# A chunked delta rule before an FFN: chunks 0 and 1 solved by 16x16 blocks and three accumulating products

## The chip, the cores and the metric

The kernel runs on one core of a Trainium2 chip. Its time is the device time of one execution in microseconds; a single program on one core, so there is no second core to compare. The engines are TensorE (PE; its weight loads are PEld in the profile), VectorE (DVE), ScalarE (ACT), GpSimd (POOL) and SyncE (SP), which here only issues DMAs.

## What is computed

For each of 4 batches and 8 heads, 768 steps with a state of 48x48, then an FFN over the 3072 rows (384 wide, 1536 hidden):

```python
k_n = k / (norm(k, axis=-1) + 1e-06)
for t in range(S):
    y[:, :, t] = q[:, :, t] @ state
    v_old = state.T @ k_n[:, :, t]
    state = state + beta[:, :, t] * outer(k_n[:, :, t], v[:, :, t] - v_old)
...
xn = x / rms(x) * rms_g
out = (silu(xn @ w_gate) * (xn @ w_val)) @ w_out
```

k, q, v, beta and the output are float32 in the kernel; the three weight matrices arrive as float64 and are converted on the chip.

## The kernel before

**Chunks.** The 768 steps are 12 chunks of 64 (C). Inside a chunk the state's corrections solve a unit triangular system of 64x64 for each of the 32 heads: with N the negative, strictly lower part of K K^T scaled by beta, the rows wanted are M r, where M is the inverse times beta and r is v less what the old state gives. `prep` (from L598) makes M, `recur` (from L844) applies it: `mr` (M r, L912), the output y (`pu`, L926), the state (`ku`, L963), the root mean square and the transposed, scaled rows `xf`, the FFN's input.

**prep.** K is scaled by 1/norm (in chunk 0 on VectorE, L646, and before that the raw scores are scaled by it, L624), transposed on TensorE (`turn`, L529) and multiplied by itself (`scores`, L552). The two diagonal 32x32 blocks of each head go through DRAM (`dkk`) into `at_`, one block per partition. VectorE then substitutes: scaling by beta (L671), pairs of rows (L696 to L706), and 15 steps of a product (L718) and a sum (L724) on `acc`. The result goes through DRAM (`dx`) into `mt` (the two diagonal blocks of M) and `x2bd`. For chunks 0 and 1 (`early`) TensorE turns the first block (L776) into `m1bd`; two products (L800, L824) make the block below the diagonal of M. For chunks 2 to 11 `m1bd` is loaded by DMA instead.

**The FFN.** Chunks 0 and 1 are multiplied plainly (`ffn_plain`: up L1101, down L1083), in two halves of the hidden width, so that half the weights suffice at first. From chunk 2 on, weight sums are formed (`factors`, `out_factors`), and the FFN runs with fewer products (L1194, L1251).

**Weights.** 18 loads of 768 KB arrive in three raw buffers in `more`. Each is converted by one ScalarE step (L473) and three VectorE steps (L461 to L469); for the first three (NPE) TensorE adds the two parts by an identity product (L486, L487) and ScalarE copies them out (L491), for the others VectorE adds them (L494).

**What sets the order.** Every operation is first given to a planner (`Plan`) with an engine, a price, a priority and its dependences; the planner writes out one fixed order for each engine. A DMA's `after` is a time in the planner's own clock before which it isn't placed; on the chip the queue takes the DMAs in their written order, each as soon as its semaphores allow. Most DMAs are issued by SP, a few of chunk 0 by ScalarE's queue. Until 70 us of the planner's clock the gaps on TensorE are filled with products of the identity (`filler`, L1354), which compute nothing that is used. TensorE takes its instructions in order, fillers among them.

Of the kernel before, what the change touches and what calls it, by code (L numbers as in the profile page):

```python
# [11 lines left out]
FP32 = mybir.dt.float32  # L12
# [6 lines left out]
C = 64  # L19
W = 32  # L20
DP = 64
# [30 lines left out]
def fillers(a, b):  # L52

    if a == 0.0:
        return [4, 4, 4, 1]
    n, t = [], a
    while t < b - 0.3:
        n.append(4 if b - t > 1.5 else 2 if b - t > 0.9 else 1)
        t += 0.22 * n[-1] + 0.02
    return n  # L60
# [195 lines left out]
def kernel(  # L256
# [42 lines left out]
    bk = sbt("bk", [128, W])  # L299
    mhalf = sbt("mhalf", [128, 2])  # L300
    zero = sbt("zero", [128, 1])
# [8 lines left out]
    NPE, NRAW, NCV = 3, 3, 2  # L310
# [20 lines left out]
    kraw = pt  # L331
    at_ = sbt("at", [128, W, W])
    acc = sbt("acc", [128, 4, W // 2, W])
    xs_ = [acc[:, 1], wflat[:, 2048:2560].rearrange("p (i t) -> p i t", t=W), wflat[:, 2560:3072].rearrange("p (i t) -> p i t", t=W)]
    xt_ = acc[:, 2].rearrange("p i t -> p (i t)").rearrange("p (k i) -> p k i", i=W // 2)
    m1bd = sbt("m1bd", [128, 16, 2, W])
    x2bd = sbt("x2bd", [128, 8, 4, W])
    mt = [sbt("mt", [128, 16, C]), wflat[:, 1024:2048].rearrange("p (x t) -> p x t", t=C)]
# [25 lines left out]
    dx = [dram.tile([2, 2, 16, W, W], FP32, name=f"dx{i}") for i in range(2)]  # L364
    dxt = [dram.tile([W, 2, 16, W], FP32, name=f"dxt{i}") for i in range(2)]
# [14 lines left out]
    def due(c, lead):  # L380

        return (64.0 - min(lead, 64.0)) if c == 0 else (90.0 if c == 1 else 160.0 + PERIOD * (c - 2)) - lead


    def setup():
# [24 lines left out]
        for keys, t in (  # L410
            ([("m1bd", g, bb) for g in range(2) for bb in range(2)], m1bd),
            ([("x2bd", y_) for y_ in range(4)], x2bd),
        ):
            n = 1
            for e in t.shape[1:]:
                n *= e
            P.add("POOL", 0.05 + 0.0009 * n, lambda t=t: nc.gpsimd.memset(t, 0.0), 1, w=keys)
        for i in range(2):
            P.add("POOL", 1.0, lambda t=mt[i]: nc.gpsimd.memset(t, 0.0), 1, w=[("mt", i, h_, bb, g) for h_ in range(3) for bb in range(2) for g in range(2)])

    def load_small():
        for i in range(8):
            src = beta.rearrange("b (y g) (c i t) -> i g (b y) c t", i=2, g=2, t=W)[i // 2 % 2, i % 2]
            dma(beta_b[16 * i : 16 * i + 16], src, 0.5, w=[("beta", i)], work=0.2, after=7.5)
        dma(g_sb, moe_rms_g.rearrange("(t p) -> p t", p=128), 1, w=["g"], after=8.0)
# [6 lines left out]
    def weights():  # L432
# [14 lines left out]
        for n, (dst, src, keys) in enumerate(todo):  # L447
# [4 lines left out]
            dma(rdst, src, (0.1 if n == 0 else 3 + 2 * n), w=[("raw", i)], dur=0.7, work=3.06, after=(7.5, 5.0, 19.2, 27.2, 24.5, 33.3, 47.0)[n] if n < 7 else 48.8)  # L452
# [25 lines left out]
            if n < NPE:  # L478
                for x_ in range(2):
                    ps = Group()  # L480
                    cut = slice(2 * x_, 2 + x_)
                    flat = slice(512 * x_, 512 + 256 * x_)
                    m = 512 - 256 * x_
# [5 lines left out]
                    P.add("PE", 0.0035 * m, s6, pr, r=cvk + cak + ["ident"], w=[("cvp", n, x_)], ps=ps, size=8)  # L489
                    done.append(("cv", n, x_))  # L490
                    P.add("ACT", A(m), lambda dst=dst[:, cut], ps=ps, m=m: nc.scalar.copy(dst, ps.t[:, 0:m].rearrange("p (a n) -> p a n", n=256)), pr, r=[("cvp", n, x_)], w=[done[-1]], last=ps)  # L491
# [9 lines left out]
    def load(c, what):  # L501
        t0 = c * C
        pk, pq, pv = ((-5, 1, 12), (5, 29, 36))[c] if c < 2 else (due(c, 150), due(c, 99), due(c, 70))
        if "q" in what and c > 1:
            for d, eh, g, th in itertools.product(range(2), repeat=4):
# [3 lines left out]
                dma(q2t[r0 : r0 + 32, :, g, th, 0 : e1 - e0], src, pq, w=[q2k[8 * d + 4 * eh + 2 * g + th]], work=0.2, after=53.2)  # L509
# [88 lines left out]


    def prep(c):  # L600
        early = c < 2
        pr = 8.0 if c == 1 else due(c, 110)
        if c == 0:
            pr = 0.0
# [785 lines left out]
```

## Time and profile before

| What | us |
|---|---|
| median of 3 runs | 705.16 (703.76 to 706.37) |
| the profiled execution | 705.78 |
| its span | 704.1 |
| TensorE busy | 687.3 |
| VectorE busy | 556.3 |
| first up-projection of the FFN (first row of L1101) | 73.37 |

In the rows of the profile, a line is: the kernel's line, engine, operation, output <- inputs, shape and count. TensorE's timeline gives the start, the length of a merged piece, and in brackets how long the engine was idle before it and what ended that. A float32 product is two TensorE records, each with a weight load of its own. The weight loads by form give busy us and the mean ns of one. Clock and matmul ends are modelled in the profile, so pitches are read from starts.

### The profile page before, as it was taken

Reading aid. Unit: us, or ns where it says so; the run is one execution under the profiler, and the core shown is the slowest. Engines: PE = TensorE matmul, PEld = TensorE weight load, DVE = VectorE, ACT = ScalarE, POOL = GpSimd, SP = SyncE. Lnnn points to the kernel's source line nnn. Section 1 sums busy time; section 2 is a strip of 40 time slices with the busy share of each in tenths; the row PEclk is TensorE's granted clock in tenths of the full one; section 3 lists DMA queues with packets and bytes.
Section 4 is the critical chain, followed back from the end, with each engine's and each line's share of the span. In section 5 each row is a group of like instructions: output and inputs, shape, how many; then the busy total and the mean of one; then the engine's idle time right before and its main releaser. Section 6 shows DMA issues by size and latency. Waiting matters only on the chain. (4 is left out here: it accounts for less than half of the span.)

```text
span 704.1 us, 23246 instructions
## 1 busy us (share of the span) xinstructions
PE 687.3 (98%) x9956; PEld 623.0 (88%) x9956; DVE 556.3 (79%) x1149; ACT 307.3 (44%) x735; POOL 139.8 (20%) x140
## 2 busy tenths in 40 slices
PE   9998989999999999999999999899999999999997
PEld 6657767777789999999999999899999999999997
DVE  4799979999799869789579669979769779648373
ACT  5434643444335446345445444246445435236241
POOL 4202111104212033213113033303033210000000
PEclk9999999999999999999999999999999999999999
DMA  7967796743612531633611442442541430210000
GB/s 144 239 129 170 154 254 127 165 69 58 111 23 44 93 58 24 104 66 54 105 34 24 81 77 48 80 76 40 83 74 22 74 71 3 45 33 2 23 1 24
DMA packets 232791, 54.67 MB, mean 78 GB/s; under 512 B 221936, under 2 KB 225008, under 8 KB 232688
## 3 DMA queue, kind: packets, MB, share of 16 engines
q1 hardware_dynamic: 227840, 52.27, 39.1%
q10 hardware_dynamic: 4848, 0.92, 0.8%
q8 instruction: 78, 1.28, 0.8%
q14 instruction: 25, 0.20, 0.1%
HBM read 40.83 MB, written 12.32 MB: 75 GB/s over the span
## 5 line engine op out<-in xcount | busy, mean ns | idle before, releaser
L1194 PE MATMUL bank<-xf,w_in 128*128 128x128 f32 x1440 | 180.4, 277 | 2.5 <-ACT tmp L1206 2.5
L1194 PEld LDWEIGHTS bank<-xf,w_in 128*128 128x128 f32 x1440 | 169.8, 192 | 5.3 <-ACT tmp L1206 2.7
L1204 DVE TENSOR_TENSOR tmp<-tmp,bank 128x512 f32<-128x512 f32 x180 | 121.3, 682 | 57.7 <-PE bank L1194 51.8
L1194 PE MATMUL bank<-xf,more 128*128 128x128 f32 x960 | 124.3, 277 | 0.0
L1194 PEld LDWEIGHTS bank<-xf,more 128*128 128x128 f32 x960 | 115.3, 192 | 1.6 <-issue 0.2
L1206 ACT COPY tmp<-bank 128x512 f32<-128x512 f32 x120 | 68.7, 585 | 93.0 <-PE bank L1194 66.0
L1210 ACT ACTIVATE tmp<-tmp 128x256 f32<-128x256 f32 x120 | 49.9, 418 | 94.7 <-DVE tmp L1204 94.4
L724 DVE TENSOR_REDUCE acc<-acc 128x30 f32<-128x90 f32 (+4 forms) x180 | 85.1, 473 | 6.2
L574 POOL TENSOR_TENSOR knrm<-ksum,half 128x16 f32<-128x16 f32 x12 | 35.6, 2968 | 166.7 <-DVE ksum L573 166.7
L718 DVE TENSOR_TENSOR acc<-acc,at 128x60 f32<-128x60 f32 (+4 forms) x180 | 62.4, 346 | 4.6 <-POOL at L701 1.7
L1251 PE MATMUL bank<-wo_sb,hf 128*128 128x192 f32 x360 | 63.9, 327 | 1.2 <-ACT xf L1038 1.0
L1251 PEld LDWEIGHTS bank<-wo_sb,hf 128*128 128x128 f32 x360 | 58.2, 190 | 1.8 <-ACT xf L1038 1.2
L1211 DVE TENSOR_TENSOR hf<-tmp 128x256 f32<-128x256 f32 x120 | 50.4, 435 | 6.5 <-ACT tmp L1210 5.9
L1354 PE MATMUL bank<-ident 128*128 128x128 f32 (+2 forms) x156 | 44.7, 433 | 1.4 <-POOL ident masks.py:199 1.4
L1354 PEld LDWEIGHTS bank<-ident 128*128 128x128 f32 x156 | 26.6, 196 | 18.1 <-issue 15.2
L671 POOL TENSOR_TENSOR at<-at,beta_b 128x1024 f32<-128x1024 f32 x8 | 19.6, 2450 | 105.1 <-DMA at<-dkk 51.8
L1260 DVE TENSOR_TENSOR tmp<-tmp,bank 128x192 f32<-128x192 f32 x30 | 10.5, 350 | 31.9 <-PE bank L1251 30.8
L1083 PE MATMUL bank<-wo_sb,hf 128*128 128x384 f32 x96 | 34.9, 495 | 0.0
L1101 PE MATMUL bank<-xf,w_in 128*128 128x256 f32 x144 | 34.1, 386 | 0.6 <-ACT xf L1038 0.6
L1101 PE MATMUL bank<-xp,w_in 128*128 128x256 f32 x144 | 33.5, 382 | 0.0
L745 POOL COPY acc<-acc 128x128 f32<-128x128 f32 x40 | 21.4, 564 | 60.7 <-DVE acc L724 60.2
L1101 PEld LDWEIGHTS bank<-xf,w_in 128*128 128x128 f32 x144 | 26.5, 190 | 5.4 <-ACT xf L1038 0.9
(167 smaller groups left out, 1018.9 us busy)
## 6 DMA issues: line engine op xcount, KB each, us to landing
at<-dkk SPq DMA_DIRECT2D x23, 256.0 KB, 4.4
more<-in_moe_w_val_dram SPq DMA_DIRECT2D x6, 768.0 KB, 5.8
more<-in_moe_w_gate_dram SPq DMA_DIRECT2D x6, 768.0 KB, 7.3
more<-in_moe_w_out_dram SPq DMA_DIRECT2D x6, 768.0 KB, 8.8
vt<-in_v_dram SPq DMA_DIRECT2D x24, 192.0 KB, 4.4
out_dram<-tmp SPq DMA_DIRECT2D x48, 96.0 KB, 2.2
k<-in_k_dram SPq DMA_DIRECT2D x23, 192.0 KB, 4.0
mt<-dx SPq DMA_DIRECT2D x84, 32.0 KB, 2.1
```

Source lines behind the costliest of these rows:

```text
L574: P.add("POOL", 2.95, lambda: nc.gpsimd.tensor_tensor(out=knrm[i2], in0=ksum[i2], in1=half, op=ALU.pow), pn, r=[("ksum", i2), "half"], w=[ ...
L718: nc.vector.tensor_tensor(out=acc[:, 1:3, 0:n, j + 2 : W].rearrange("p a i t -> p i a t"), in0=acc[:, old, 0:n, j : j + 2, None].to_broadc ...
L724: nc.vector.tensor_reduce(out=acc[:, new, 0:n, j + 2 : W], in_=acc[:, lo : lo + 3, 0:n, j + 2 : W].rearrange("p a i t -> p i t a"), axis=A ...
L1083: nc.tensor.matmul(po[p].t[:, 0:DM], hf[:, spot(f), 128 * p : 128 * p + 128], wo_sb[:, spot(f)], start=(f == f0), stop=(f == f1 - 1), skip ...
L1101: nc.tensor.matmul(ps.t[:, TOK * side : TOK * side + TOK], w_in[:, side, h_, 3 * t + i_, n : n + 128], x_[:, 2 * t : 2 * t + 2].rearrange( ...
L1194: nc.tensor.matmul(g.t[:, 128 * z : 128 * z + 128], fac[:, side, 128 * f : 128 * f + 128], xf[:, xs], start=(begin and z == 0), stop=False ...
L1204: P.add("DVE", V(512), lambda t=t, g=g: nc.vector.tensor_tensor(out=t, in0=t, in1=g.t, op=ALU.add), -1, r=[g], w=[tk], last=g)
L1206: P.add("ACT", A(512), lambda t=t, g=g: nc.scalar.copy(t, g.t), -1, r=[g], w=[tk], last=g)
L1210: P.add("ACT", A(256), lambda t=t: nc.scalar.activation(out=t[:, 0:256], in_=t[:, 0:256], func=ACTF.Silu), -1, w=[tk])
L1211: P.add("DVE", V(256), lambda t=t, f0=f0, p=p: nc.vector.tensor_tensor(out=hf[:, spot(f0) : spot(f0) + 2, 128 * p : 128 * p + 128], in0=t[ ...
L1251: nc.tensor.matmul(g.t[:, 0:192], a_[:, f], b_[:, f], start=(begin and f == 0), stop=(f == 5), skip_group_check=True)
L1354: nc.tensor.matmul(warm[:, 0 : 128 * w_].rearrange("p (w n) -> p w n", n=128), ident, ident[:, None, :].to_broadcast([128, w_, 128]))
```

## The change

Chunks 0 and 1 get a function of their own, `prep16`; `prep` keeps chunks 2 to 11 and loses its `early` branches. The strict part below the 16x16 diagonal blocks is not inverted any more: with D the inverse of the diagonal blocks and E = D N, both of each head's 64x64, u = D r is followed by three rounds of u = D r + E u, each written as a product with the last change that accumulates in the same bank. Two heads share one 128x128 block-diagonal tile (`nbd` for N, `ebd` for E).

```diff
+L = 16
-        return [4, 4, 4, 1]                      # fillers before the first work
+        return [4, 4, 1]
-    NPE, NRAW, NCV = 3, 3, 2
+    NPE, NRAW, NCV = 4, 3, 2
...
-due(c): 160.0 + PERIOD * (c - 2)
+due(c): 162.0 + PERIOD * (c - 2)
...
-        beta after=7.5, g after=8.0
+        beta after=2.0, g after=27, and b16: beta by 16x16 blocks, two ScalarE copies
-        weights after=(7.5, 5.0, 19.2, 27.2, 24.5, 33.3, 47.0)[n] if n < 7 else 48.8
+        weights after=(1.4, 29.5, 35.9, 33.7, 36.0, 38.0, 39.5)[n] if n < 7 else 52.9
-        q, k of chunk 1 and v: after=1.4, 27.2; 8.6; 34.4, 41.2; later q and k 53.2
+        q, k of chunk 1 and v: after=18.2, 45; 5.9; 14.0, 44.7; later q and k 46.5
```

Beside the diff's own lines above, the changed tables are given in one line each. The planner's price of a TensorE conversion also changes. The new function, cut:

```diff
+    def prep16(c):
+        if c == 0:
+            turn(kn, kt[0], ktk, kkeys + kp, pr, True)          # K not scaled by its norm
+            ps = scores(kt[0], kt[0], pr, ktk, ...)
+            kraw = -scores                                      # one VectorE, one ScalarE copy
+            bk = (1/norm by block) * (1/norm by block) * b16[:, 0]
+        else:
+            kd scaled by krec on GpSimd; turn; scores; n0 = -scores (ScalarE)
+        for g in range(2):
+            dma(dk[g].rearrange("x j t -> j x t"), full[64 * g : 64 * g + 64], ...)      # 256 KB each
+            nbd[rows, :, 64 * g : 64 * g + 48] = full[rows, :, 0:48] * below             # GpSimd
+        if c == 0:
+            vt = vt * knrm[0]                                   # VectorE, 128x768
+        for r0, b0, n in place:                                 # four loads of 16x16 blocks
+            dma(a16[c][r0 : r0 + W], dk...[:, b0 : b0 + L, b0 : b0 + L], ...)
+        scale (128x256), share1, share3, share2 (128x128)       # VectorE
+        for j in range(0, L - 2, 2):                            # seven steps
+            n, m = j + 2, L - 2 - j
+            nc.vector.tensor_tensor(out=acc[:, 1:3, 0:n, cols]..., op=ALU.mult)
+            nc.vector.tensor_reduce(out=acc[:, new, 0:n, cols], ..., op=ALU.add)
+        spread: two ScalarE copies into x16[c]
+        for r0, b0, n in place:
+            dma(dm...[:, b0 : b0 + L, b0 : b0 + L], x[r0 : r0 + W], ...)     # dm was zeroed by one 512 KB store
+        for g in range(2):
+            dma(dg[c][64 * g : 64 * g + 64], dm[g].rearrange("x s t -> s x t"), ...)
+        if c:
+            four more loads of dm into mt[1]
+        for h in range(2):
+            for bb in range(2):
+                for y_ in range(4):
+                    nc.tensor.matmul(ps.t[:, n : n + 64], nbd[:, x_], dg[c][:, x_])       # coupling
+            ebd <- ps, on the diagonal; half by VectorE, half by ScalarE (64x512 each)
```

In `recur`, for c < 2 (chunk 0 in two halves h, chunk 1 in one):

```diff
+        def couple(h, t):
+            for p in h:
+                for bb in range(2):
+                    for y_ in range(4):
+                        nc.tensor.matmul(psu[bb, p].t[:, n : n + 48], ebd[:, x_], t[:, x_], start=False, stop=True, ...)
...
         for h in halves:
+            first product: first_rows(h) for c == 0 (dg and v), mr(h) otherwise
+            evacuate(h, c > 1)                                  # u <- bank
+            if c > 1:
+                continue
+            for n in range(3):
+                P.add("PE", 0.7 * len(h), couple(h, zb if n else u_), ...)
+                if n < 2:
+                    change(h)                                   # zb = bank - u, VectorE
+                if n == 0:
+                    evacuate(h, False, ("ACT", "ACT"))
+            evacuate(h, True)
```

Removed for chunks 0 and 1: the 32x32 substitution, `dkk`, `dx`, `x2bd`, `turn_m11` (L776), the two merging products (L800, L824) with their copies, and in chunk 0 the second transposes and scores of the scaled K. GpSimd clears the shared tile `mx` (ebd, and m1bd with x2bd for the later chunks) again after chunk 1.

## Prediction

> **What bounds the kernel now.** I read the page first, then the table of engine time by stage, TensorE's timeline over the first 110 us, VectorE's timeline beside it, and the weight loads by form.
>
> ```profile
> PE 687.3 (98%) x9956; PEld 623.0 (88%) x9956; DVE 556.3 (79%) x1149; ACT 307.3 (44%) x735; POOL 139.8 (20%) x140
> ```
>
> TensorE is busy for 98% of the span, but not with work all the time. Its timeline tells the two apart:
>
> ```profile
> 28.97 9.85 PE L1354 MATMUL bank<-ident 128*128 128x512 f32 x28
> ...
> 46.02 8.13 PE L1354 MATMUL bank<-ident 128*128 128x512 f32 x24
> ...
> 61.11 1.41 PE L912 MATMUL bank<-vt,mt 64*64 64x48 f32 x64
> ...
> 73.37 4.15 PE L1101 MATMUL bank<-xf,w_in 128*128 128x256 f32 x18 [0.64 <-ACT xf L1038]
> ...
> 103.15 0.32 PE L926 MATMUL bank<-u,pt 64*64 64x48 f32 x5 [2.20 <-issue]
> ```
>
> L1354 is filler. Up to the first up-projection at 73.37 TensorE spends 41 us on fillers (177 blocks of 128 columns), 7 us idle and about 25 us on work; in the 630.7 us behind it, it is idle for 11. So the end moves with two things only: when the first up-projection starts, and how much TensorE work lies behind it. The start waits for chunk 0's substitution on VectorE, between these rows (13.3 us; scaling and pairs from 25.39 make it 16.6), and for its stores and loads:
>
> ```profile
> 28.72 0.22 DVE L718 TENSOR_TENSOR acc<-acc,at 128x60 f32<-128x60 f32 x1
> ...
> 41.73 0.28 DVE L724 TENSOR_REDUCE acc<-acc 128x30 f32<-128x90 f32 x1
> ```
>
> **The price that decides.** The rest of the triangle is now three products with ebd (`couple`), each a full 128x128 weight tile with only 48 moving columns, and the tiles come from products with nbd (64 moving columns). Every fp32 product is two records with a weight load each. No row of before has a full tile with so few columns, so I bound it. These are weight loads by form, with the mean in ns last:
>
> ```profile
> L1194 PEld LDWEIGHTS bank<-xf,w_in 128*128 128x128 f32 x1440 | 169.8, 192 | 5.3 <-ACT tmp L1206 2.7 <-issue 1.0 <-ACT tmp L1296 0.2
> L552 PEld LDWEIGHTS bank<-kt 64*64 64x64 f32 x832 | 13.7, 134 | 4.4 <-issue 2.7 <-ACT kt L541 0.7 <-DVE tmp L1204 0.5
> L800 PEld LDWEIGHTS bank<-m1bd,kk 128*32 128x32 f32 x352 | 5.4, 109 | 2.9 <-issue 2.0 <-DMA q<-in_q_dram 0.2
> ```
>
> 192, 134 and 109 ns for 128, 64 and 32 columns: 0.86 ns per column, so 128 columns need some 0.11 us. A matmul that follows other work, its load unhidden, against one in a run (timeline):
>
> ```profile
> 26.28 0.70 PE L486 MATMUL bank<-xf,ident 128*128 128x512 f32 x1
> ```
>
> ```profile
> 16.86 0.59 PE L487 MATMUL bank<-more,ident 128*128 128x512 f32 x1
> ```
>
> Again 0.11 us is what an exposed load adds. And from the chain of waits the pitch in a run:
>
> ```profile
> 493.00 0.87 PE bank L529 x8
> ...
> 664.01 21.44 PE bank L1194 x192
> ...
> 685.45 1.95 PE bank L1251 x12
> ```
>
> 0.109 us for 128 moving columns (L529), 0.1625 for 192 (L1251): 0.00084 per column. Lower end, the load fully hidden: 0.042 for 48 columns, 0.055 for 64. Upper end, each record waits for its load: 0.1117, L1194's pitch (load and stream not overlapped at all is excluded: L1194 would then be near 0.22). There are 96 + 32 new products, half per chunk: 192 + 64 records, 11.5 us by the lower end, 28.6 by the upper. I take the upper: the load's slope and the exposed 0.11 are both of full tiles, and a next load cannot hide behind a 0.04 us stream.
>
> The Trainium skill, "TensorE: Matmul & The Clock Gate", has both rules: section "LDWEIGHTS (loading the stationary operand)" gives columns / 1.2 in ns, 107 for 128 columns, and the table in "Back-to-back issue gap" gives about 60 cycles, 25 ns, for up to 64 moving columns. Estimates from that page: 27.3 us for the new products by the first rule, 6.4 by the second, which would make the whole 708 or 688; the rows above side with the first, against this change.
>
> **Part by part, up to the first up-projection.** TensorE's queue in the changed kernel's instruction order, up to its first w_in product, holds:
> - the start, 1.4, and 9 filler blocks at the first fillers' slow rate (13 took 5.5): 3.8;
> - 104 more filler blocks at 0.217 (45 took 9.7 from 28.97): 22.6;
> - old work by its rows: eight k, q and k1 transposes each 0.87, scores 1.09 + 1.05 + 1.1, norms 0.2, two conversions 5.3 (26.28 to 28.97 is one), first product 1.08, y 1.1, state 0.7, transposes 0.66: 14.9. Chunk 0's second transposes and scores, L776, L800 and L824 are gone;
> - new, chunk 0's half: 14.3.
>
> That is 57.0 without any wait. Now the chain. K goes out unscaled after one 0.69 copy behind the scores (near 10.3) instead of two 0.65 scalings behind the reciprocal (12.25). The two 256 KB stores should land in about 4 (a 192 KB k load: 4.0), by 14.5. The four block loads move 64-byte pieces, 512 each: nearest are dxt (1024 such pieces, 2.7) and the contended block load on ScalarE's queue (6.0).
>
> ```profile
> dxt<-acc SPq DMA_DIRECT2D x20, 64.0 KB, 2.7
> ...
> at<-dkk ACTq DMA_DIRECT2D x1, 256.0 KB, 6.0
> ```
>
> Two of them stand on ScalarE's queue behind w_in copies that wait for the first weight conversion, and v, the zeros and q (1.3 MB) follow on SP, so I take 20 (18 to 22). Substitution: scale and pairs 1.2 (256 elements 0.41, L1109), then seven steps of 28 to 64 outputs at the pitch of L718 with L724 (0.55 at 30, 0.69 at 56): 4.5. Stored out near 26.4, landed 29.6, back as one tile 34 (4.0 again). TensorE's queue reaches the coupling at 33, so this chain and the fillers end nearly together. The three rounds are then TensorE's own: one half's 1.8 us of products covers the other half's change (2 x 0.36 on VectorE) and copies (2 x 0.4 on ScalarE); at the lower price some 0.8 a round would be bare. First y product near 52.6; from there 8.4 by L988, L1013, L1021, L1034 and L1038 (10.7 in before, with a 1.15 stop and fillers). So the first up-projection is at **61**, that is 4 of waits on 57, where before has 5.5.
>
> Covered: VectorE's v scaling (1.1), the b16 copies, GpSimd's nbd products (four of about 1.5, L646) and its memsets end before 17; if a nbd product ended after 33 the coupling would slip by as much. The block zeros after chunk 1 (1.9) are wanted only near 140. Loads released anew: weight 1 now goes out behind the tile load, near 30, and lands at 36 to 41; VectorE wants it near 43; each us later moves the start by one. Weights 2 and 3 go near 33; in VectorE's order chunk 1's substitution (5.8, saving 11 there) stands before their conversions, done by 62 and 64 against a need at 65 and 69.
>
> **Behind it.** 630.7, plus a conversion that was done before (n=2) and one moved from VectorE (n=3), 5.3; q1's transposes and scores, 2.0; chunk 1's new products 14.3, less L776, L800 and L824, 2.2; less 2.0 for the stop at 103.15, which stands behind runs of small records that become fewer (0 at the other end): 648.1. Chunks 2 to 11 keep their instructions. VectorE's net saving, about 17 us (two substitutions from 33.2 to 11.4, 10 of new copies, changes and v scaling against 5 of old ones), is off the path: TensorE covers it.
>
> **Sum:** 61 + 648.1 = 709.1 against a span of 704.1, so 5.0 us longer. The profiled execution took 705.78 in all; the median of the runs is 705.16, so I say 710.2.
>
> **Rivals.**
> - *The load hides* (faster): the streams set the pitch, 0.042 and 0.055. The queue then holds 48.5, waits grow to 5, start 53.5; behind it 639.6. 693.1, or 694.2 as a median. For: rows with smaller tiles pass at 0.017. Against: four of them load side by side, and the 0.11. Between the ends the sum is a line, and it crosses 704.1 where the 256 records average 0.091 us; below that the change wins.
> - *No difference*: the price as forecast, but no waits up to the start (57) and 3.7 less idle behind it: 703.4, 704.5 as a median. For: VectorE has 17 us less to do. Against: 5.5 of waits in before.
> - *The stores and loads come late*: the block loads or the tile at the contended 6.0 to 7.0, the tile back near 39. Start 66, 714.1, 715.2 as a median. For: v, zeros and q in the same queues. Against: no weight load beside the chain.
>
> **Chances:** forecast 0.50, load hides 0.20, no difference 0.17, late 0.13. The forecast alone reaches from 706 to 714, and 0.06 of it lies below 708.7. Half a per cent, 3.5 us, is about what a measurement of this kernel can tell from no change: slower 0.57, same 0.23, faster 0.20. The range runs from 694 to 717, taking in both ends of the price.
>
> **What will show it.** The pitch of the 48-column records: 0.11 or 0.04. The first up-projection at 61. VectorE's first substitution in under 6 us, from about 20. TensorE idle for 9 to 12 behind the start. I am wrong if those records pass below 0.09, or if TensorE idles anew behind the start.

## The result and the profile after

| | before | after |
|---|---|---|
| median of 4 runs each, us | 704.46 (703.03 to 706.37) | 733.46 (731.79 to 736.18) |
| ratio | | 1.0414 (95%: 1.0366 to 1.0461) |
| the profiled execution, its span | 705.78, 704.1 | 736.18, 734.5 |
| first up-projection (first row of L1101, L1282 after) | 73.37 | 84.09 |
| behind it | 630.7 | 650.4 |
| mean granted clock | 0.999 | 0.967 |

Slower by 29 us; 710.2 was forecast. Behind the first up-projection the forecast was 648.1, and it is 650.4. The miss is in the start: 84.09 instead of 61. These are two lines of the page of after, TensorE's busy time and the granted clock in 40 slices of 18 us.

```profile
PE 719.2 (98%) x9858; PEld 658.1 (90%) x9858; DVE 537.6 (73%) x1129; ACT 304.9 (42%) x733; POOL 148.9 (20%) x147
...
PEclk9965899899999999999999999999999999999999
```

The share of busy time is 98% again and tells nothing. The second line does: the clock is at 6 and 5 tenths in the third and fourth slice, where it was full in before. TensorE's timeline of after shows what ran there:

```profile
41.58 5.12 PE L780 MATMUL bank<-mt,wsum 128*128 128x64 f32 x32 [1.78 <-DMA mt<-dm]
46.63 3.65 PE L1056 MATMUL bank<-vt,mt 64*64 64x48 f32 x64
...
50.80 6.90 PE L1067 MATMUL bank<-u,mx 128*128 128x48 f32 x32
...
58.91 6.90 PE L1067 MATMUL bank<-state,mx 128*128 128x48 f32 x32
...
66.16 6.90 PE L1067 MATMUL bank<-state,mx 128*128 128x48 f32 x32
...
84.09 4.15 PE L1282 MATMUL bank<-xf,w_in 128*128 128x256 f32 x18
...
109.09 3.68 PE L780 MATMUL bank<-kk,wsum 128*128 128x64 f32 x32
...
115.14 3.77 PE L1067 MATMUL bank<-u,mx 128*128 128x48 f32 x32
```

L1067 is `couple`, a round of 32 records. For chunk 1 (115.14) it takes 3.77, for chunk 0 6.90, nearly twice as long, with nothing idle inside. The engine time by stage, cut at the edges at which the clock changes, confirms that this is the clock (after the busy times: granted clock, DMA share, GB/s):

```profile
40.30:43.72 3.42, 2.14 (x19) 2.17 (x20) 0.06 (x1) 0.00 (x0) 0.00 (x0) 1.00 1.11 312
43.72:47.13 3.41, 3.41 (x25) 3.29 (x26) 1.01 (x2) 0.58 (x1) 0.28 (x1) 0.50 0.93 263
...
53.96:57.37 3.41, 3.41 (x18) 3.41 (x17) 0.62 (x2) 0.54 (x2) 0.00 (x0) 0.50 0.00 0
...
74.44:77.85 3.41, 3.41 (x51) 1.65 (x53) 0.00 (x0) 0.76 (x2) 0.00 (x0) 0.50 0.88 158
77.85:81.26 3.41, 3.41 (x100) 2.77 (x96) 1.69 (x7) 3.21 (x13) 1.10 (x2) 1.00 0.24 46
```

From 43.72 to 77.85, ten stretches of 3.41 us, the clock is exactly half. (Between the ends of each trace, every piece that the clock stays at one value is a multiple of 3.41 us long, at a phase of its own.) Half clock also comes for one stretch at 16.4, at 118.8 (behind a stretch that a round of chunk 1 filled without a gap) and for two at 142.7. Undisturbed, the weight load is what the forecast said. The loads by form, mean ns last but for the idle times:

```profile
L1375 PEld LDWEIGHTS bank<-xf,w_in 128*128 128x128 f32 x1440 | 170.7, 192 | 3.4 <-DVE tmp L1385 1.0 <-issue 0.6 <-ACT tmp L1387 0.4
...
L1067 PEld LDWEIGHTS bank<-state,mx 128*128 128x128 f32 x64 | 13.9, 333 | 0.0
...
L1067 PEld LDWEIGHTS bank<-r,mx 128*128 128x128 f32 x64 | 7.4, 192 | 0.3
```

192 ns for chunk 1's tiles, as for any full tile; 333 for chunk 0's. The second thing in the start is VectorE's timeline:

```profile
11.80 1.79 DVE L614 TENSOR_SCALAR knrm<-knrm 128x16 f32<-128x16 f32 x1
...
13.80 2.48 DVE L503 SCALAR_TENSOR_TENSOR tmp<-more,tmp 128x768 f32<-128x768 uint32 x1
...
25.75 0.42 DVE L705 TENSOR_TENSOR at<-at,bk 128x256 f32<-128x256 f32 x1 [8.10 <-DMA at<-dfull]
...
31.39 0.27 DVE L748 TENSOR_REDUCE acc<-acc 128x28 f32<-128x84 f32 x1
```

The substitution itself takes 5.9 us (25.75 to 31.66), as forecast, but starts at 25.75 instead of 20, after 8.1 us of waiting for its loads. And two operations in front of it are odd: L614 takes 1.79 for 128x16 elements (0.16 for chunk 1, at 31.58). The DMA view (median us from issue to landing last):

```profile
dfull<-pt SPq DMA_DIRECT2D x1, 256.0 KB, 4.9
...
mt<-dm ACTq DMA_DIRECT2D x1, 256.0 KB, 5.8
at<-dfull SPq DMA_DIRECT2D x6, 32.0 KB, 5.2
dm<-at SPq DMA_DIRECT2D x6, 32.0 KB, 1.9
at<-dfull ACTq DMA_DIRECT2D x2, 32.0 KB, 4.9
```

SP issued its two block loads of chunk 0 at 17.06, ScalarE's queue its two at 20.12, behind the copies of the first conversion (L524), the second of which starts at 20.05.

### The profile page after: what moved, and what is told of

Read it like the earlier page. It is cut to its first block, busy times and chain, and to the rows that moved or that the text cites. A ratio compares the mean times of both kernels' runs of the same rounds, so it can differ in the third digit from the quotient of the medians.

```text
span 734.5 us, 23017 instructions
## 1 busy us (share of the span) xinstructions
PE 719.2 (98%) x9858; PEld 658.1 (90%) x9858; DVE 537.6 (73%) x1129; ACT 304.9 (42%) x733; POOL 148.9 (20%) x147
## 4 chain that ended last, share of the span: by engine, by line
PE 85%; DVE 7%; DMA 4%; SPq 2%; ACT 1%; issue 1%; ACTq 0%; DVEq 0%
PE bank L1375 36%; PE bank L1432 19%; PE bank L1282 6%; PE bank L1067 4%; PE bank L995 3%; PE bank L589 3%; PE bank L1264 2%; SPq L389 2%; PE bank L1077 2%; PE bank L1042 1%; PE bank L566 1%; PE bank L780 1%; DMA more<-in_moe_w_gate_dram 1%; PE bank L520 1%; DVE acc L887 1%; PE bank L1215 1%
## 5 line engine op out<-in xcount | busy, mean ns | idle before, releaser
L1375 PEld LDWEIGHTS bank<-xf,w_in 128*128 128x128 f32 x1440 | 170.7, 192 | 3.4 <-DVE tmp L1385 1.0
L1375 PE MATMUL bank<-xf,more 128*128 128x128 f32 x960 | 125.9, 278 | 0.0
L887 DVE TENSOR_REDUCE acc<-acc 128x30 f32<-128x90 f32 (+4 forms) x150 | 71.0, 473 | 5.2
L881 DVE TENSOR_TENSOR acc<-acc,at 128x60 f32<-128x60 f32 (+4 forms) x150 | 51.0, 340 | 6.6 <-POOL at L864 5.0
L1282 PE MATMUL bank<-xp,w_in 128*128 128x256 f32 x144 | 35.6, 402 | 0.0
L1282 PE MATMUL bank<-xf,w_in 128*128 128x256 f32 x144 | 35.3, 396 | 0.0
L1282 PEld LDWEIGHTS bank<-xp,w_in 128*128 128x128 f32 x144 | 28.6, 202 | 5.5 <-DVE hf L1290 0.3
L1282 PEld LDWEIGHTS bank<-xf,w_in 128*128 128x128 f32 x144 | 28.0, 198 | 5.4 <-issue 0.2
L907 POOL COPY acc<-acc 128x128 f32<-128x128 f32 x40 | 19.6, 521 | 64.5 <-DVE acc L887 64.3
L1538 PE MATMUL bank<-ident 128*128 128x512 f32 (+2 forms) x90 | 30.4, 484 | 1.4 <-POOL ident masks.py:199 1.4
```

Source lines behind the costliest of these rows:

```text
L881: nc.vector.tensor_tensor(out=acc[:, 1:3, 0:n, j + 2 : W].rearrange("p a i t -> p i a t"), in0=acc[:, old, 0:n, j : j + 2, None].to_broadc ...
L887: nc.vector.tensor_reduce(out=acc[:, new, 0:n, j + 2 : W], in_=acc[:, lo : lo + 3, 0:n, j + 2 : W].rearrange("p a i t -> p i t a"), axis=A ...
L1282: nc.tensor.matmul(ps.t[:, TOK * side : TOK * side + TOK], w_in[:, side, h_, 3 * t + i_, n : n + 128], x_[:, 2 * t : 2 * t + 2].rearrange( ...
L1375: nc.tensor.matmul(g.t[:, 128 * z : 128 * z + 128], fac[:, side, 128 * f : 128 * f + 128], xf[:, xs], start=(begin and z == 0), stop=False ...
L1538: nc.tensor.matmul(warm[:, 0 : 128 * w_].rearrange("p (w n) -> p w n", n=128), ident, ident[:, None, :].to_broadcast([128, w_, 128]))
```

## The experiments

**Theories.** *A*: records that are bound by their weight load and stream few columns lower the clock by themselves. *B*: the stops of TensorE ahead of the coupling (1.62 and 1.78 us) lower it, whatever is multiplied. *C*: the clock has no part; the products' price and the late chain are the cause. "Start" is the first up-projection in the profiled execution, "behind" the rest of its span, before on the same chips 704.93 to 706.11. In e2 to e7, e11 and e12 VectorE, ScalarE, GpSimd and SP have the instructions of after in the same order, so that only TensorE's products differ.

| run | median, us | ratio, 95% | start | behind |
|---|---|---|---|---|
| after | 733.46 | 1.037 to 1.046 | 84.09 | 650.4 |
| e4_no_idle | 717.03 | 1.013 to 1.020 | 67.43 | 648.2 |
| e5_wide | 715.91 | 1.012 to 1.021 | 66.01 | 648.3 |
| e11_wide64 | 715.3, 715.7, 731.4, 735.4 (each) | | 66.89 | 647.0 |
| e3_fill_between | 734.97 | 1.038 to 1.047 | 82.73 | 649.8 |
| e6_twice48 | 747.59 | 1.055 to 1.062 | 95.33 | 651.7 |
| e7_twice64 | 729.56 | 1.030 to 1.037 | 77.19 | 650.1 |
| e2_tiles64 | 707.70 | 1.000 to 1.005 | 65.36 | 643.1 |
| e12_nbd_late (the same program as e2) | 706.43 | 1.000 to 1.004 | 63.66 | 643.0 |
| e8_sp_loads | 710.66 | 1.005 to 1.010 | 60.67 | 651.5 |
| e9_npe3 | 706.64 | 0.998 to 1.004 | 62.99 | 642.6 |
| e10_combined | 711.95 | 1.006 to 1.011 | 62.67 | 647.8 |
| e13_nbd_after | 704.97 | 0.996 to 1.000 | 69.58 | 636.7 |
| e14_v_after | 705.75 | 0.997 to 1.002 | 69.68 | 636.0 |
| e15_v_after_npe3 | 709.70 | 1.004 to 1.010 | 70.56 | 635.4 |

### No stop ahead of the coupling

```diff
             def coupling(h=h, ps=ps):
+                if not c and not h:
+                    filler([4, 4, 4])
```

> Three filler blocks (2.6 us) go ahead of chunk 0's coupling, where TensorE stops for 1.8 us. Theory A (the run of few-column products does it): the clock falls all the same, at most one window of 3.4 us later, and the time stays within 731 to 736. Rival B (the stop does it): the clock holds through the coupling and the rounds, 17 us go and about 0.8 comes: 717 to 720.

717.03: B's number. TensorE's timeline of this run:

```profile
41.12 3.68 PE L782 MATMUL bank<-mt,wsum 128*128 128x64 f32 x32
...
47.05 3.67 PE L1069 MATMUL bank<-u,mx 128*128 128x48 f32 x32
...
51.28 3.67 PE L1069 MATMUL bank<-state,mx 128*128 128x48 f32 x32
...
55.08 3.67 PE L1069 MATMUL bank<-state,mx 128*128 128x48 f32 x32
...
67.43 4.15 PE L1284 MATMUL bank<-xf,w_in 128*128 128x256 f32 x18
```

The same products, each round 3.67 instead of 6.90, the start 16.7 us earlier, the rest of the span nearly as it was (648.2 for 650.4). So the clock is worth 16.4 us of the 29 (733.46 less 717.03, the three fillers included), and C falls. A, as I had put it, falls too: the same run of few-column products passed at full clock.

### More columns under the same weight loads

```diff
-    nc.tensor.matmul(ps.t[:, n : n + 64], nbd[:, x_], dg[c][:, x_])
+    nc.tensor.matmul(ps.t[:, n0_ : n0_ + 128], nbd[:, x_], dg[c].rearrange("p x t -> p (x t)")[:, f0 : f0 + 128])
...
-    nc.tensor.matmul(psu[bb, p].t[:, n : n + 48], ebd[:, x_], t[:, x_], ...)
+    nc.tensor.matmul(psu[bb, p].t[:, n : n + 128], ebd[:, x_], t.rearrange("p x e -> p (x e)")[:, f0 : f0 + 128], ...)
```

> Chunk 0's products with ebd and nbd each stream 128 moving columns instead of 48 or 64 (the neighbouring columns too, so the values of chunk 0's rows are not the reference's); the number of records and of weight loads is the same, and each does more. Theory A (the clock is halved because too few columns stream under each weight load): at full clock a record with 128 columns passes in 0.11 to 0.12 us, as one with 48 does, so with more work per record the kernel gets faster: the clock stays above 0.9, a round takes 3.6 to 3.9 instead of 6.9, first up-projection near 67 to 70, 716 to 720 in all. Rival C, or any in which the products' own cost is what lengthens the start: 733 or more, since no record gets cheaper by streaming more. Rival B (the stop ahead of the coupling): half clock at 43.7 still, rounds of 6.9, 733.

715.91, though each product streams twice to nearly three times as much and the stop of 1.74 us ahead of the coupling is still there. The clock stays full, a round takes 3.74. That is A's number, and B falls: the stop alone does not do it either. Engine time in the stretch with the stop, to be set beside 40.30:43.72 of after:

```profile
37.47:40.88 3.41, 2.15 (x19) 2.18 (x20) 0.02 (x1) 0.00 (x0) 0.00 (x0) 1.00 1.10 303
```

TensorE is busy for 2.15 us with 19 records, as in after (2.14, 19), and yet the next stretch is at full clock here. Some quantity that both the stop and the few columns lower must decide.

### Fillers between the products

```diff
+                        if not c and y_ == 3:
+                            filler([4])          # in coupling and in couple
```

> One filler block of 512 moving columns goes between every four products of chunk 0's coupling and of its three rounds: 16 blocks, 0.87 us each at full clock, 13.9 us of added work. Theory A (few moving columns per record are what lowers the clock): the clock stays full, the rounds cost 3.6 each beside their fillers; some 17 us of half clock go and 13.9 come: 728 to 733, and the granted clock between 44 and 78 us is above 0.9. Rival B (the stops ahead of the coupling do it, and the run only goes on at half clock): the clock falls as before and the fillers pass at half speed too until it is given back: 745 to 760. Rival C (no part for the clock): 747.

734.97, with start 82.73. The clock falls behind the stop (1.59 us) for one stretch of 3.41 us, at 42.5, and is full in the rounds: won back as soon as fillers run between, at the price of the fillers. B's 745 and C's 747 are out; A's 733 was missed by that one stretch.

**Theory D.** In every trace I counted the moving columns that TensorE streamed in each stretch of 3.41 us between possible clock changes, each record's spread over its time up to the start of the next record. A stretch full of fillers counts 4096. In after, the stretch from 40.30, with the stop in it, counts 1214, those at half clock in the rounds 768 to 1284, and the one from 115.40, full of a round of chunk 1 with no stop, 1472; all are followed by half clock. In the run without the stop the lowest of the rounds counts 1627 and keeps it; in the run with 128 columns the stretch above counts 2377. So D: below some 1620 columns in a stretch the next runs at half clock, above it at full. A run of 48-column records at 0.112 us streams 1465: too few by itself, saved in the run without the stop only by the 128 to 256 columns of filler between rounds. At half clock it streams half of that (768 counted) and did not win the clock back.

### The same products twice, 48 or 64 columns

```diff
+            for _ in range(2):
+                nc.tensor.matmul(psu[bb, p].t[:, n : n + 48], ebd[:, x_], ...)   # the other run: 64
```

Both with the three fillers ahead of the coupling, so without a stop.

> The kernel with the three filler blocks ahead of chunk 0's coupling (717.0 us, full clock in the whole start), and in it every product of chunk 0's three rounds is made twice (the second adds the same again, so chunk 0's values are not the reference's). A round is then a run of 64 records of 48 columns, 7.2 us at full clock, with no stop in it. New theory D, from counting the moving columns in each clock window of 3.41 us over all runs so far: a window that streams 1615 columns or fewer is followed by a window at half clock, one with 1627 or more by one at full clock; a run of records with 48 columns at 0.112 us streams 3413 / 112 x 48 = 1465 per window at full clock and half that at half clock, so it lowers the clock by itself as soon as it fills a window, and cannot win it back. D: the clock falls within the first round and stays at half to the end of the third; rounds 2 and 3 at 13.8 us each; 739 to 749 in all. Rival B (only a stop of TensorE lowers the clock): full clock throughout, 96 records more at 0.112: 717.0 + 10.8 = 728.

> The same, with 64 moving columns in each of those products instead of 48 (16 columns of the neighbour are added to, so chunk 0's values are not the reference's). As many records and weight loads as in the run with 48, and more streamed in each. Theory D: 3413 / 112 x 64 = 1950 columns per window are above the bound, the clock stays full: 717.0 + 10.8 = 726 to 730, some 10 to 20 us faster than with 48 columns. Rival A (any run of records bound by their weight load lowers the clock): as with 48 columns or slower, 739 or more. Rival B: 728 here and 728 with 48 columns.

747.59 with 48 columns and 729.56 with 64: more work per record is 18 us faster, as D has it on both sides; B wanted 728 twice, A 739 or more twice. Engine time by stage with 48 columns:

```profile
47.90:51.31 3.41, 3.41 (x33) 3.41 (x32) 0.62 (x2) 0.54 (x2) 0.06 (x1) 1.00 0.21 18
51.31:54.73 3.42, 3.42 (x19) 3.42 (x17) 0.00 (x0) 0.00 (x0) 0.00 (x0) 0.50 0.02 5
...
58.14:61.55 3.41, 3.41 (x18) 3.41 (x17) 0.00 (x0) 0.00 (x0) 0.00 (x0) 0.50 0.00 0
```

and with 64:

```profile
47.60:51.01 3.41, 3.41 (x33) 3.41 (x32) 0.62 (x2) 0.34 (x2) 0.00 (x0) 1.00 0.23 18
51.01:54.42 3.41, 3.41 (x32) 3.36 (x30) 1.50 (x4) 0.84 (x3) 0.00 (x0) 1.00 0.02 7
```

The first rows are alike to the last record: TensorE and its weight loads busy for all of 3.41 us, 33 records. Only the columns differ (1461 and 1956 counted), and only the first is followed by half clock.

### 64 columns with the stop

The change is that of the run with 128 columns, with 64 in the rounds only.

> The changed kernel with 64 instead of 48 moving columns in chunk 0's three rounds (16 columns of the neighbour are added to, so chunk 0's values are not the reference's); coupling, stops and everything else as they are. Theory D: the stop ahead of the coupling lowers the clock as before, and at half clock a record takes 0.215 us, so a window streams 3413 / 215 x 64 = 1016 columns, below the bound of about 1620: the half clock stays to the end of the rounds, 730 to 737, the same as with 48. With 64 columns and no stop the clock had held (729.6 with the products made twice). Rival: the time falls in the proportion of the columns streamed; between 48 (733.5) and 128 (715.9) that is 730 at most, or the clock comes back as it did with 128: 716 to 720.

The four executions took 715.3, 715.7, 731.4 and 735.4 us at mean granted clocks of 1.000, 0.996, 0.977 and 0.967. D, as I had put it, is right for two of the four. In the profiled one (715.7) the stop was 1.32 us and fell so that its stretch still counted 1611 columns, and the clock stayed. The edges of the stretches do not move with the kernel (the last one ahead of the coupling lies at 40.30 in after, at 39.25 in this profile), so how much of the stop falls into one stretch differs from one execution to the next. That this parted the four is inferred: the two long ones have no trace, only their mean clocks, and that of the longest is after's. With 48 columns and the stop none of the four executions of after escaped (731.8 to 736.2). The rival that wanted a time in proportion to the columns has none.

### 64x64 tiles

```diff
-    nc.tensor.matmul(psu[bb, p].t[:, n : n + 48], ebd[:, x_], t[:, x_], ...)
+    for g in range(2):
+        rows = slice(64 * g, 64 * g + 64)
+        nc.tensor.matmul(psu[bb, p].t[rows, n : n + 48], ebd[rows, x_, rows], t[rows, x_], ...)
     # coupling alike
```

> Every product with ebd and nbd, of both chunks, is split into its two diagonal 64x64 blocks (the other two quarters of those tiles are zeros), nothing else changes. Theory A (the full tiles' products run at one weight load each, and a long run of them with only 48 or 64 moving columns makes the chip halve TensorE's clock): 64x64 products pass at 0.022 us a record as in the first product of before (1.41 us for 64), so a round falls from 6.9 to 1.4 us and a coupling half from 2.5 to 0.7; the clock stays near full up to the first up-projection; that starts near 61 (84.1 less 16.4 for rounds, 3.9 for the coupling, 6 for other work that ran at half clock, plus some 3 of waits between the rounds that are then bare); behind it 640 to 642 instead of 650.4. In all 701 to 706. Rival B (the stops of 1.6 and 1.8 us ahead of the coupling halve the clock, whatever the products are): the clock still falls at 43.7 and the work behind it runs at half speed for some windows; start near 66, 706 to 710. Rival C (the time is the price of full tiles and the late chain, the clock has no part): the rounds shrink likewise, but first product, conversions and fillers keep their 6 us: 707 to 711.

707.70, above A's 701 to 706 and where B and C had it. But not for their reasons: the clock holds through coupling and rounds, with a stop of 1.36 ahead of them. Timeline of TensorE:

```profile
39.93 2.08 PE L782 MATMUL bank<-mt,wsum 64*64 64x64 f32 x64 [1.36 <-DMA mt<-dm]
...
44.22 2.07 PE L1071 MATMUL bank<-u,mx 64*64 64x48 f32 x64
...
51.59 0.84 PE L1071 MATMUL bank<-state,mx 64*64 64x48 f32 x21 [0.63 <-issue]
...
58.06 0.51 PE L1148 MATMUL bank<-u,k 64*48 64x48 f32 x25 [2.20 <-issue]
...
65.36 4.15 PE L1286 MATMUL bank<-xf,w_in 128*128 128x256 f32 x18
```

A round of twice as many records takes 2.07 instead of 3.67, 0.032 a record. Against the run without the stop the 64x64 tiles are worth 9.3 us (717.03 less 707.70). A's start was 61, not 65.36. Its sum began from after's own 84.1, so the late chain was in it; too low was the price, 1.4 us for a round and as much for the coupling, where 2.07 and 2.08 were measured (2.7 us over the four), and it had neither the two stops without a releaser (0.63 and 2.20) nor the stretch of half clock from 59.20 to 62.62. B and C had the number, so the time alone does not part the theories here; the clock in the rounds does.

### The late chain

Chunk 0's substitution still starts at 24.38 with 64x64 tiles, where 20 was forecast for after. First, the block loads all on SP:

```diff
-    dma(a16[c][r0 : r0 + W], ..., eng=next(turns), ...)
+    dma(a16[c][r0 : r0 + W], ..., eng="SP", ...)
```

> The kernel with 64x64 tiles (707.7 us, first up-projection at 65.4), and chunk 0's four block loads all issued from SP, none from ScalarE's queue, where two of them stood behind the copies of the first conversion until 19.3 us (SP's went out at 15.8). If these two set the start of the substitution (24.4), the last of four goes out near 17.2, lands near 22.3, and the start moves by 2 us: first up-projection at 63.4, 705.7 in all, and the stops of TensorE ahead of the scores and the coupling (1.4 to 1.6 each) get shorter by as much. Rival: the loads land late because v, zeros and q are moved beside them (landing 6.3 on SP already): no gain, 707.7.

VectorE's timeline of this run has the substitution at 19.60, the forecast's 20:

```profile
19.60 0.42 DVE L705 TENSOR_TENSOR at<-at,bk 128x256 f32<-128x256 f32 x1 [2.72 <-DMA at<-dfull]
```

4.8 us earlier for the queue alone: SP's first loads go out at 15.83 (15.79 with two of the four on ScalarE's queue), and L614 and L503 are as slow as they were (1.79 and 2.49). The start gains 4.7 (60.67), and the time is 710.66, not less: behind it are 651.5 instead of 643.1. The planner wrote a new order for every engine (in the runs with 64x64 tiles that was so wherever a price or an engine changed), and this one holds stops of 2.3 and 2.7 us for VectorE. What of the 8 us is due to the order and what to the earlier start is not settled.

Then GpSimd's nbd products. The first attempt only added a key to their dependences:

```diff
-    ..., r=kkall + ["below"], w=["nbd"])
+    ..., r=kkall + ["below"] + ([] if c else ["bk"]), w=["nbd"])
```

> The kernel with 64x64 tiles, and GpSimd's two products for chunk 0's nbd wait for the norms by block (bk) as well, so they run near 15.5 to 19.5 instead of 10.7 to 14.6; the order of instructions on every engine is the same. If they are what slows VectorE's L614 (1.83 us there, 0.16 for chunk 1) and L503 (2.48), these return to 0.2 and near 1, the norms' reciprocal comes 1.7 us earlier, the first conversion's copies on ScalarE and behind them its two block loads some 2 to 3 us earlier, the substitution starts at 21.5 to 22.5 instead of 24.4, first up-projection 63 to 64 instead of 65.4, 705.5 to 706.5 in all. Rival: VectorE's two operations are slow for another reason (the wait for a DMA write or their own operands): they stay, and so does the time, 707.7.

The planner's keys set the order alone and the order came out the same, so this is e2's program once more: 706.43, and L614 at 1.81, L503 at 2.47 in it. It says how far two measurements of one program lie apart (1.3 us), and nothing on GpSimd. In the next run the products really move:

```diff
-    P.add("POOL", G(768), ...nbd..., r=kkall + ["below"], w=["nbd"])      # ahead of the block loads
+    P.add("POOL", G(768), ...nbd..., r=kkall + ["below"] + [("ab", 0, n) for n in range(4)], w=["nbd"])   # behind them
```

> The kernel with 64x64 tiles, and GpSimd's two products for chunk 0's nbd put behind the block loads in the plan, so that on GpSimd they stand behind the scaling of chunk 1's k (some 32 to 36 us, still ahead of the coupling near 40). The run before this one was to do that with a key alone; the key gave the same order and so the same program, and these products still ran at 11.2. Theory: GpSimd's products are what slows VectorE's L614 (1.81 to 1.83 us against 0.16 for chunk 1) and L503 (2.47 against 0.96): both return to these, the norms' reciprocal is ready 1.7 us earlier, TensorE's stop of 1.7 to 1.9 ahead of the norms goes, and the first conversion's copies and ScalarE's two block loads behind them come 2 to 3 us earlier (15.5 to 17 instead of 18.0 to 19.3), so the substitution starts at 21 to 22 instead of 23.3 to 24.4. Rival: VectorE's two operations are slow for another reason and stay. The order behind the start is planned anew, so the whole time may move by some us either way (700 to 709); only the start decides between the two.

VectorE's timeline:

```profile
11.24 0.17 DVE L614 TENSOR_SCALAR knrm<-knrm 128x16 f32<-128x16 f32 x1
...
11.61 0.90 DVE L503 SCALAR_TENSOR_TENSOR tmp<-more,tmp 128x768 f32<-128x768 uint32 x1
```

0.17 and 0.90 instead of 1.8 and 2.5, and ScalarE's loads go out at 15.99. The theory on GpSimd holds; the substitution did not come earlier, since the planner now put the scaling of v ahead of it (L696, waiting for v until 23.45). That was moved in the next two runs:

```diff
-    P.add("DVE", 1.1, ...vt..., r=[("knrm", 0)], ...)            # ahead of the substitution
+    P.add("DVE", 1.1, ...vt..., r=[("knrm", 0)] + xkeys, ...)    # behind it
```

> The kernel with 64x64 tiles and the nbd products behind the block loads (705.0 us, where VectorE's scaling of v stood ahead of the substitution and waited for v until 23.5, and the first up-projection came at 69.6), and the scaling of v put behind the substitution. VectorE's order is then norms, substitution, and only then v. Expected in the start: block loads out at 16 to 16.4 on both queues, substitution from 21 to 22 (two separate effects of GpSimd and of the queue taken away together), coupling near 37, first up-projection 60 to 62, 8 to 9 earlier than in the run before. If TensorE's work behind the start alone decides (637 there, 640 to 643 in the other runs with 64x64 tiles): 699 to 705. Rival: the earlier start is given back, since VectorE (92% busy between 130 and 240 us) is what the middle waits for; then the time stays at 705 to 707 and the milestones (a quarter of the up-projections at 242) do not come earlier.

> The same, and the fourth weight conversion on VectorE instead of TensorE (2.6 us of products less there, 1 us more for VectorE). If TensorE's work decides: 2.6 less than the run before it in this call, 697 to 702. If VectorE is what the middle waits for: the same as that run or slower, 705 to 708.

The substitution starts at 19.87 and 20.03, and then runs into GpSimd again. Timeline of VectorE in the first of the two:

```profile
20.33 1.56 DVE L726 TENSOR_TENSOR at<-at 128x128 f32<-128x128 f32 x1
21.81 1.93 DVE L734 TENSOR_TENSOR acc<-acc,at 128x8 f32<-128x8 f32 x2
23.77 1.90 DVE L729 TENSOR_TENSOR at<-at 128x128 f32<-128x128 f32 x1
25.71 0.22 DVE L747 TENSOR_TENSOR acc<-acc,at 128x56 f32<-128x56 f32 x1
```

and of GpSimd beside it:

```profile
20.08 1.55 POOL L673 TENSOR_TENSOR k<-k,krec 128x768 f32<-128x768 f32 x1 [0.63 <-DVE krec L615]
21.59 3.92 POOL L689 TENSOR_TENSOR wsum<-pt,below 64x768 f32<-64x768 f32 x2
```

The same operations take 0.40, 0.25 and 0.29 in after (L721, L729, L724 there). Each VectorE operation ends only when a GpSimd one does: 21.9 beside 21.6, 23.7 and 25.7 beside the two halves of 21.6 to 25.5. The substitution takes 10.4 instead of 5.9, and the tile's loads, beside three weight loads issued at 34 to 36, let TensorE stop for 4.0 ahead of the coupling (5.9 in the second run); the clock is then half for one stretch (45.81 to 49.23) and for two in the second run. Start 69.68 and 70.56, so the forecast 61 was not reached this way, and the expected 60 to 62 was wrong. Times 705.75 and 709.70: as fast as before, no faster.

### One conversion less on TensorE

```diff
-    NPE, NRAW, NCV = 4, 3, 2
+    NPE, NRAW, NCV = 3, 3, 2
```

> The kernel with 64x64 tiles, and the fourth weight conversion (n=3) made by VectorE's addition, as in the kernel before, instead of TensorE's products with ident. TensorE loses 2.6 us of products behind the first up-projection (two pairs of 0.86 and two of 0.43), VectorE gains one addition of 1 us in a stretch where it is busy for 47 to 70%. If all TensorE work behind the start is on the path: 705.1. Rival: VectorE's conversion is then late for the products that want it: 707.7 or more.

> Three edits together: 64x64 tiles, chunk 0's four block loads all from SP, and the fourth weight conversion back on VectorE. The planner makes a new order for all engines from these. In the start I expect what the run with the loads on SP showed: substitution from about 19.6, first up-projection near 60.7 (before: 73.4). Behind it, if TensorE's work alone counts there: 643 of the run with 64x64 tiles less the conversion's 2.6, 640; together 701 and 1.7 around the span, 702.5. Rival: an earlier start is given back behind it, as in the run with the loads on SP (651 behind the start, with stops of 2.3 to 2.7 for VectorE's results): 706 to 710, no faster than the kernel before (705).

706.64, 1.06 less than the first measurement of the kernel with 64x64 tiles and no less than the second (706.43): the expected 2.6 is not shown. With the loads on SP as well 711.95, no gain at all. The waits of TensorE in the first:

```profile
PE bank L589 <- issue: 6.1, 1, 6.1
```

TensorE waits 6.1 us for nothing that the profile shows, at 108, behind some 210 records of small tiles in 5 us, and the clock is half behind that, from 110.30 to 123.95. The two kernels differ from e2 in the whole order, so that the conversion's 2.6 us can't be read from them.

## Why the prediction was wrong

**The price of the products: right.** 64 records in 7.26 us (the run with 64 columns), 0.11 each, is the upper end that was chosen. The rule of the Trainium skill for the weight load, 107 ns for 128 columns, held (section "LDWEIGHTS (loading the stationary operand)" of "TensorE: Matmul & The Clock Gate"). The 25 ns by its table in "Back-to-back issue gap" did not hold for these records; the page gives that table for the gap of single matmuls, with no time for the weight load in it.

**Behind the start: right.** 648.1 forecast, 650.4, and 648.2 and 648.3 in the two runs with full clock in the rounds. TensorE is idle for 7.6 there (11.4 in before), less than the 9 to 12 that were named.

**"The three rounds are then TensorE's own": the step that failed.** They were, but the sum priced them, the coupling, the first product, the fillers between them and part of a conversion at full clock. The forecast's own price step has 0.04 us of streaming in a record of 0.11, and did not ask what so few columns do to the clock: that term stood at nothing. The runs showed half clock from 43.72 to 77.85, at a price of 16.4 us of the miss of 23.3.

**The chain: right in kind, mis-sized by 6.4.** At full clock the start is 67.43, not 61. The coupling comes at 41.1, not 33; from there to the first y product 19.35 (19.6 forecast) and on to the up-projection 7.0 (8.4). Of the 8.1 the block loads are 4.65 (the substitution starts at 24.65 in that run, for 20): ScalarE's queue was named in the forecast, but in after its loads only went out at 20.12, when all four were to have landed. With all four on SP the substitution starts at 19.60. The rest is the way from the last step to the coupling, 9.9 in after (31.66 to 41.58) where 7.3 was forecast (25.7 to 33), and what the three added fillers take, under 1.

**"GpSimd's nbd products ... end before 17" as covered: wrong.** They end at 15.5, and VectorE pays for them meanwhile: 1.6 us on L614 and 1.5 on L503, both ahead of the copies behind which ScalarE's loads stand.

**The substitution: right.** 5.9 for 5.7. **The stop at 103.15: right**, none in after; in six of the eight runs with 64x64 tiles stops of that kind come again (1.5 to 6.1).

**The rivals.** "The load hides" fell with the price. "Stores and loads late" was true beside the forecast, not in its place. Neither sign of being wrong came, records below 0.09 or new idle time behind the start: both looked past the clock. The direction (slower) was right; that the range ended at 717 was wrong because no case had the clock in it, though at full clock the kernel lies at its edge (717.03).

**Where the gain went.** With 64x64 tiles and the clock held in the rounds, the start is 8 us earlier than before (65.36) and the rest 12.4 longer (643.1 to 630.7): by the forecast's own terms the conversions and chunk 1's products stand there instead. No version was faster than before beyond the measurement.

## What to carry to other kernels

A run of products with full weight tiles and few moving columns costs its weight loads, and beside that may cost the clock of everything near it, as here 16.4 us: work out how many columns stream in 3.4 us, not how busy the engine looks, and split block-diagonal tiles into their blocks. Look at the granted clock in stretches before explaining a longer row by anything else. An operation on GpSimd is not free because GpSimd is idle: see what VectorE does beside it.

## What the runs showed of the hardware

**The clock follows the columns streamed, not idleness.** Over 1697 stretches of 3.41 us in all sixteen traces in which TensorE had full 128x128 tiles only (two small-tile records at most): all 33 with up to 1604 columns were followed by half clock, all 1662 with 1627 or more by full clock, and the two between (1611 and 1615) fell one to each side. That is 0.39 to 0.40 of the 4096 of a full stretch. (With each record's columns spread over its whole modelled time the counts part between 1550 and 1564.) At full clock, stretches up to 1517 lost it and those from 1611 kept it; at half clock, those up to 1615 stayed there and those from 1649 won it back, so that the two bounds, if they differ, lie close together. In stretches with 64x64 tiles, of which up to four start within 20 ns (34.52 to 34.54 in after), this count is no measure. The Trainium skill ("TensorE: Matmul & The Clock Gate", section 'Part 1: The HAM clock gate (the "warmup" mystery)') has the stretch, 3413 ns and free-running, and the half rate, which agree; it ties half rate to an idle window, and here stretches without any idle time lost the clock (1461 and 1472 columns) while one with 1.4 us of it kept it (from 30.06 in after, 2168 columns).

**GpSimd holds VectorE up.** VectorE's small operations took 1.5 to 1.95 us beside a GpSimd product of two operands and 0.17 to 0.43 without, each time to about the end of GpSimd's own instruction: L614 1.78 to 1.83 in all twelve traces in which GpSimd's nbd product started just ahead of it, and 0.17 in the three in which that product was moved. The Trainium skill ("SBUF — State Buffer", section "SBUF: two separate sides") says of these two engines that they take a shared pair of ports in turn, one instruction at a time, for a VectorE operation with two inputs in that memory or in a mode that uses two ports. L726, L734 and L503 have two inputs and agree. L614 has one tensor input and was held up too (1.79 in after); whether it ran in such a mode no run here shows.

**Stops of TensorE with no releaser, behind small records.** Such stops ("issue") of 1.5 to 6.1 us stand in or behind long runs of records of 64x64 tiles, in before (2.2) and in six of the eight runs with 64x64 tiles. In the longest, the trace has a transfer of 16 KB on the queue of instructions at 111.2, 2.0 us long, and TensorE goes on at 114.4. In all 16 stops of this kind of 1 us or more, in all the traces, it goes on 1.2 to 1.8 us after the end of such a transfer; that it waited for these transfers is likely and was not tested.
